# A fused sketch-attention and MoE kernel: two loads issued later, a transpose moved, GpSimd products gated behind VectorE, and a new placement of the attention steps between the MoE waves

## The chip, the cores and the metric

The kernel runs on one core of one Trainium2 chip. The metric is device time in microseconds for one launch; lower is better. The engines of the core work side by side, each through its own instruction queue in program order: TensorE (PE in the profile, its weight loads as PEld), VectorE (DVE), ScalarE (ACT), GpSimd (POOL) and SyncE (SP), which here issues nearly all DMA transfers.

## The reference

Two stages, and the second one takes the output of the first.

```python
def phi(x):                       # r = 8 sketches, their outer product: 64 features
    a = np.einsum('rd,bhsd->bhsr', S1, x)
    b = np.einsum('rd,bhsd->bhsr', S2, x)
    return np.einsum('bhsi,bhsj->bhsij', a, b).reshape(*x.shape[:-1], r * r)

q_p, k_p = phi(q), phi(k)         # q, k, v: (4 batches, 4 heads, 1088 rows, 32)
kv = np.einsum('bhsf,bhsd->bhfd', k_p, v)
z = np.sum(k_p, axis=2)
num = np.einsum('bhsf,bhfd->bhsd', q_p, kv)
den = np.einsum('bhsf,bhf->bhs', q_p, z)[..., None] + 1e-06
attn = num / den

x = attn.transpose(0, 2, 1, 3).reshape(4352, 128)
h = x @ w_in                      # w_in: (128, 2048)
g = h * (1.0 / (1.0 + np.exp(-beta * h)))
out = g @ w_out                   # w_out: (2048, 128)
```

All inputs and the output are float32.

## The kernel before

**Attention, one batch at a time.** The 1088 rows of a head are cut into 34 blocks of 32 rows, called u. `k_turn` and `q_turn` (L313, L319) transpose the loaded k and q on VectorE in 32 by 32 blocks; `k_project` and `q_project` (L338) apply both sketches on TensorE into two PSUM banks of the tag "att", and two VectorE transposes (L349) bring the result back as `ab`. `k_product` (L365) forms the outer products of k, one part on VectorE and one on GpSimd; `v_copy` (L326) puts v into the layout that `kv` (L384, TensorE) needs. `kv_spread` (L394, L398), `weights` (L408, L416) and `kv_repeat` (L426 on TensorE, L434 on ScalarE) turn kv and z into operands. `den_rows` (L440) and `den_product` (L454 to L459) with `den_invert` and `weigh` (L470, L471, L486) give q's factors divided by the denominator, `an`. Then for each of three chunks of the batch `q_multiply` (L504, a product) and `q_back` (L512, a transpose) make the features of q, and `num` (L524) multiplies them with kv on TensorE. `evacuate` (L585) writes the result to `x_all` in fp16.

The first chunk of batch 0 goes another way, so that its x is there early: its numerator is made without the division (`num_first`, copied to `ns` at L548), the reciprocals are spread by a selector matrix on TensorE (`quotient`, L556), and a VectorE product (L565) joins both into `x_all`. In this chunk `q_multiply(0)` and `q_back(0)` do not need the denominator.

**MoE in waves.** The 136 blocks of all batches are cut into ten chunks of 12, 11, 11, then six of 16, and 6 blocks. beta is folded into the weights: `winp` is w_in times beta (GpSimd, L276), `woutp` is w_out over beta (GpSimd L291, ScalarE L285). A chunk of the first nine has eight waves. A wave is two first matmuls (L635) into a pair of PSUM banks ("wave", two such pairs), one ScalarE activation (L642) to `gT`, and, two waves later, two second matmuls (L611) into the accumulator bank. A chunk ends with a VectorE transpose (L616) and its stores (L622).

**Order.** It is written out by hand; no scheduler moves anything. Up to the first wave the order is the source order (L643 to L720). From then on a table `plan` has one dictionary for each batch: the number behind a step is its due time in waves. After wave n (waves counted from 1) every step whose due time is below n is issued, in order of due time. Every engine gets its instructions in that order, so a step that is issued early stands in front of later work in its queue, and a wait in it holds up all that is behind. Slots that are not in the table are not run.

**Loads.** A `load_…` first puts a small memset on the destination (`hold`, L120), which ties the load to that point of VectorE's queue, and then issues the transfer on SP's queue. SP takes its transfers in order, so one that waits for its memset holds back the ones behind it.

**Gates.** `in_turn(one, other)` writes the same small tile `gate` on two engines, one after the other (L126, L127); the second engine goes on only when the first one has got there.

**Fillers.** `warm(n)` issues n matmuls on a tile of zeros (L221) whose result is not used; they stand in TensorE's queue in program order. `kv`, `k_project`, `q_project`, `kv_repeat`, `den_rows` and `num_part` all take banks of the two "att" ones, so each has to wait until the reader of the bank's last tile is done.

Of the kernel before, what the change touches and what calls it, by code (L numbers as in the profile page):

```python
# [18 lines left out]
def kernel(  # L19
# [19 lines left out]
    nc = tc.nc  # L39
# [10 lines left out]
    C = 9  # L50
# [58 lines left out]
    UH = U // 2 + 1  # L109
# [9 lines left out]
    def hold(eng, t):  # L119
        eng.memset(t[:, 0:1], 0.0)  # L120
# [4 lines left out]
    def in_turn(one, other):  # L125
        one.memset(gate, 0.0)  # L126
        other.memset(gate, 0.0)  # L127

    def load_w_in():
        nc.sync.dma_start(out=w_in_sb, in_=moe_w_in)  # L130
        nc.sync.dma_start(out=betat, in_=moe_beta.rearrange("(p j) -> p j", j=NJ))
# [5 lines left out]
    def load_k(b, eng, u0=0, u1=U):  # L137
        hold(eng, k_in[b][:, u0 * D : u1 * D])
        nc.sync.dma_start(out=k_in[b][:, u0 * D : u1 * D], in_=k_rows[b][:, u0 * D : u1 * D])

    def load_q(b, eng):
        hold(eng, q_in[b])
        nc.sync.dma_start(out=q_in[b], in_=q_rows[b])

    def load_v_late(b, eng):
        hold(eng, v_in[b].rearrange("p h c d -> p (h c d)"))
        load_v(b)
# [71 lines left out]
    def warm(n):  # L219
        for _ in range(n):  # L220
            nc.tensor.matmul(  # L221
                out=idle_out[:, 0:NI], lhsT=idle[:, 0:P], rhs=idle[:, 0:NI], start=True, stop=True
            )
# [50 lines left out]
    def scale_w_in(j0, j1):  # L274
        for j in range(j0, j1, 2):
            nc.gpsimd.tensor_tensor(  # L276
                out=winp[:, j : j + 2, :],
                in0=apx(w_in_sb, j, [[1, 2], [NJ, P]]),
                in1=apx(beta_bc, j * P, [[P, 2], [1, P]]),
                op=ALU.mult,  # L280
            )

    def scale_w_out_act(j0, j1):
        for j in range(j0, j1):
            nc.scalar.activation(  # L285
                out=woutp[:, j, :], in_=w_out_sb[:, j, :], func=ACTF.Copy, scale=rbetat[:, j : j + 1]
            )
# [364 lines left out]
    at = [Attention(b) for b in range(B)]  # L652
    a0 = at[0]
# [7 lines left out]
    sketch_rows()  # L661
    warm(2)
    a0.k_project((0, 1))
    load_k(1, nc.vector, 0, UH)
    load_w_in()
    a0.k_turn((1,))
    a0.k_project((2, 3))
    warm(10)
# [3 lines left out]
    for i in range(2):  # L672
# [2 lines left out]
    sketch_columns()  # L675
    warm(3)
    a0.k_product(nc.vector, 0, 4)
    in_turn(nc.vector, nc.gpsimd)
    a0.q_turn()
    a0.k_product(nc.gpsimd, 7, C)  # L680
# [8 lines left out]
    a0.q_multiply(0)  # L689
    load_w_out(nc.vector)  # L690
    in_turn(nc.vector, nc.gpsimd)
    a0.q_back(0)
    scale_w_in(0, 10)
    warm(2)
    load_k(1, nc.vector, UH, U)
# [3 lines left out]
    a0.kv_repeat((0,))  # L699
    a0.den_rows(0, 1)  # L700
    a0.kv_repeat((1,))
    at[1].k_turn((0,))
    a0.den_product(0, 1)
    a0.den_invert(0, 1, rz[:, :, 0:H])
    a0.spread_rden()
    nc.vector.reciprocal(out=rbetat, in_=betat)
    a0.num_first()
    warm(3)
    a0.quotient()
    load_v_late(1, nc.vector)  # L710
    a0.den_rows(1, NCH, idle_out[:, NI:512])
# [10 lines left out]

    slots = []
    plan = [
        {"wo3": 1, "wo5": 2.3, "wo7": 6.1, "mul1": 0.4, "back1": 1.8, "mul2": 0.45, "back2": 1.85, "num": 5.65, "ev": 5.7},
        {"turn_k": 3.5, "proj_k": 6.4, "vcopy": 5.1, "kp_pool": 9.1, "turn_q": 3.8, "kp": 6.65, "proj_q": 7.2, "kv0": 9.15, "kv1": 9.2, "spread": 9.25, "weights": 9.3, "repeat": 18.4, "den": 9.35, "inv": 9.4, "mul0": 12.65, "back0": 15.3, "mul1": 15.3, "back1": 15.65, "mul2": 15.75, "back2": 18.1, "num": 22.5, "ev": 22.55},
        {"load_k": 0, "load_q": 3.65, "load_v": 14, "turn_k": 7.8, "turn_q": 11.95, "vcopy": 20.3, "proj_k": 19.15, "kp_pool": 23.35, "kp": 20, "proj_q": 23.3, "kv0": 24.6, "kv1": 24.65, "spread": 25.3, "weights": 26.95, "repeat": 35.4, "den": 27, "inv": 27.45, "mul0": 28.1, "back0": 32.05, "mul1": 31.55, "back1": 33.2, "mul2": 33.1, "back2": 36.15, "num": 38.65, "ev": 38.7},
        {"load_k": 16.4, "load_q": 8.7, "load_v": 29.6, "turn_k": 23.4, "turn_q": 24.45, "vcopy": 36.6, "proj_k": 37.55, "kp_pool": 40.5, "kp": 38.2, "proj_q": 39, "kv0": 41.85, "kv1": 41.9, "spread": 43.35, "weights": 43.4, "repeat": 49.1, "den": 44.05, "inv": 45.1, "mul0": 48.25, "back0": 49.2, "mul1": 48.3, "back1": 50.75, "mul2": 50.65, "back2": 54.3, "num": 54.65, "ev": 54.85},
    ]
    for b, steps in enumerate(plan):  # L730
        a = at[b]
        ch0 = 1 if b == 0 else 0
        do = {
            "load_k": lambda b=b: load_k(b, nc.vector),
            "load_q": lambda b=b: load_q(b, nc.vector),
            "load_v": lambda b=b: load_v_late(b, nc.vector),
            "turn_k": lambda a=a, b=b: a.k_turn((1,) if b == 1 else (0, 1)),
            "turn_q": a.q_turn,
            "vcopy": lambda a=a: a.v_copy(nc.gpsimd.tensor_copy),
            "proj_k": a.k_project,  # L740
            "proj_q": a.q_project,
            "kp_pool": lambda a=a: a.k_product(nc.gpsimd, 6, C),
            "kp": lambda a=a: a.k_product(nc.vector, 0, 6),
            "kv0": lambda a=a: a.kv((0,)),
            "kv1": lambda a=a: a.kv((1,)),
            "spread": a.kv_spread,
            "weights": a.weights,
            "repeat": a.kv_repeat,
            "den": lambda a=a: (a.den_rows(0, NCH), a.den_product(0, NCH)),
            "inv": a.weigh,  # L750
            "num": lambda a=a, ch0=ch0: a.num_part(ch0, NCH),
            "ev": lambda a=a, b=b: a.evacuate("VVAA" if b else "AVAA"),
        }
        for ch in range(NCH):
            do[f"mul{ch}"] = lambda a=a, ch=ch, e=nc.gpsimd if b == 1 and ch == 1 else None: a.q_multiply(ch, e)
            do[f"back{ch}"] = lambda a=a, ch=ch: a.q_back(ch)
        for i in range(NJ // 2):
            do[f"wo{i}"] = lambda i=i: scale_w_out_act(2 * i, 2 * i + 2)
        slots += [(w, b, do[step]) for step, w in steps.items()]
# [39 lines left out]
```

## Time and profile before

| | |
|---|---|
| median of 3 runs | 111.91 us (111.76 to 112.13) |
| the profiled execution's own time | 113.0 us |
| its span, first to last instruction | 111.3 us |
| mean granted TensorE clock | 0.978 |
| PE busy | 101.0 us (91%) |
| ACT busy | 76.4 us (69%) |
| DVE busy | 69.3 us (62%) |
| POOL busy | 27.8 us (25%) |
| first wave starts | 19.02 us |
| last ScalarE activation starts | 106.30 us |

The page gives busy times and a picture of the span in 40 slices of 2.78 us; a digit is the busy share of a slice in tenths. Matmuls overlap in the records, so a full PE row says that TensorE was never without work, and not that the work could not be denser. The chain of waits goes back from the last instruction to what released it. In a row of the timeline the first number is the start in us, the second the busy time of the group; a bracket gives the idle time of the engine in front of it and what ended it. Releasers are inferred from semaphores.

By the waits of TensorE from 46 us on, it stands still once, for 0.2 us. Its waits from 19 to 46 us sum to 4.6 us: 1.7 for VectorE's transposes in front of kv, 1.5 for ScalarE in three places, 0.7 for zi, 0.4 for the transposed q products, 0.3 for wc.

### The profile page before, as it was taken

The numbers are of one execution on the slowest core, as the hardware profiler recorded it, in microseconds if no ns is written. First come the engines' busy times: TensorE is split into PE (matmuls) and PEld (weight loads), VectorE is DVE, ScalarE is ACT, GpSimd is POOL, SyncE is SP. The second block draws the span as 40 slices with busy tenths as digits, with TensorE's granted clock in tenths as the row PEclk, the third lists the DMA queues.
The fourth block names the chain that finished last, engine by engine and source line by source line (L and its number), as shares of the span: only waits on it lengthen the run. The fifth ranks groups of instructions, "written<-read, shape, count | busy, mean of one in ns | idle before, by whom it ended". The sixth has DMA issues, their size and how long they took to land.

```text
span 111.3 us, 3316 instructions
## 1 busy us (share of the span) xinstructions
PE 101.0 (91%) x1401; PEld 50.1 (45%) x1401; DVE 69.3 (62%) x136; ACT 76.4 (69%) x110; POOL 27.8 (25%) x55
## 2 busy tenths in 40 slices
PE   5998999669936999999999999999999999999960
PEld 3443865324433555446344434463443444444640
DVE  5569984996895799969589949434998220020120
ACT  0704512995620499753979986757999799999940
POOL 6505299934500050590000038200000000000000
PEclk9999999999997699999999999999999999999997
DMA  3999498575004506740221720022004105004143
GB/s 85 300 236 342 138 333 337 162 222 194 34 0 142 135 0 185 203 87 9 38 32 54 193 47 6 0 51 49 0 4 69 28 0 95 2 9 72 19 71 59
DMA packets 22407, 11.25 MB, mean 101 GB/s; under 512 B 18804, under 2 KB 20852, under 8 KB 22136
## 3 DMA queue, kind: packets, MB, share of 16 engines
q1 hardware_dynamic: 21936, 10.97, 37.3%
q8 instruction: 11, 0.18, 0.7%
q10 hardware_dynamic: 456, 0.06, 0.3%
q14 instruction: 4, 0.03, 0.1%
HBM read 8.80 MB, written 2.23 MB: 99 GB/s over the span
## 4 chain that ended last, share of the span: by engine, by line
PE 58%; ACT 18%; DVE 12%; DMA 6%; issue 2%; SPq 1%; DVEq 0%
PE wave L635 19%; PE acc L611 17%; ACT gT L642 16%; DMA q_in<-in_q_dram 6%; PE wave L524 5%; PE att L338 4%; DVE kp L365 2%; PE att L384 2%; PE att L440 2%; PE wave L384 2%; PE att L426 2%; PE acc L221 2%; DVE qp L504 2%; DVE qpt L512 2%; PE att L524 1%
## 5 line engine op out<-in xcount | busy, mean ns | idle before, releaser
L642 ACT ACTIVATE gT<-wave 128x1024 f16<-128x1024 f32 (+2 forms) x76 | 65.6, 954 | 15.3 <-PE wave L635 15.2
L635 PE MATMUL wave<-x_all,winp 128*128 128x512 f16 (+3 forms) x160 | 42.3, 351 | 1.5 <-ACT gT L642 1.5
L611 PE MATMUL acc<-gT,woutp 128*128 128x512 f16 (+3 forms) x160 | 42.0, 349 | 0.2 <-ACT gT L642 0.2
L635 PEld LDWEIGHTS <-winp 128*128 128x128 f16 x160 | 14.0, 99 | 22.0 <-issue 12.6
L611 PEld LDWEIGHTS <-woutp 128*128 128x128 f16 x160 | 15.5, 98 | 14.6 <-issue 0.4
L616 DVE STREAM_TRANSPOSE osb<-acc 128x512 f32<-128x512 f32 (+3 forms) x10 | 6.3, 630 | 18.2 <-PE acc L611 18.2
L326 POOL COPY vc<-v_in 96x256 f32<-96x256 f32 (+2 forms) x8 | 6.2, 810 | 21.5 <-DMA v_in<-in_v_dram 21.5
L512 DVE STREAM_TRANSPOSE qpt<-qp 128x768 f32<-128x768 f32 x12 | 11.1, 953 | 0.0
L349 DVE STREAM_TRANSPOSE ab<-att 128x288 f32<-128x288 f32 x16 | 6.7, 458 | 4.7 <-PE att L338 4.6
L221 PE MATMUL acc<-idle 128*128 128x320 f16 x39 | 8.0, 346 | 1.3 <-DVE idle L156 1.3
L365 DVE TENSOR_TENSOR kp<-ab 128x1536 f32<-128x1536 f32 (+2 forms) x5 | 8.6, 1727 | 0.7 <-DVE ab L349 0.5
L365 POOL TENSOR_TENSOR kp<-ab 128x768 f32<-128x768 f32 (+1 forms) x4 | 7.2, 1791 | 4.6 <-DVE ab L349 4.6
L504 DVE TENSOR_TENSOR qp<-an,ab 128x768 f32<-128x768 f32 x8 | 7.7, 984 | 0.1
L524 PE MATMUL wave<-qpt,kvw 32*32 32x288 f32 (+2 forms) x192 | 7.3, 344 | 0.5 <-DVE qpt L512 0.4
L276 POOL TENSOR_TENSOR winp<-w_in_sb,beta_bc 128x256 f16<-128x256 f32 x8 | 6.6, 846 | 0.7 <-DMA w_in_sb<-in_moe_w_in_dram 0.7
L313 DVE STREAM_TRANSPOSE kT<-k_in 128x576 f32<-128x576 f32 (+1 forms) x8 | 5.6, 715 | 1.0 <-DMA k_in<-in_k_dram 1.0
L524 PE MATMUL att<-qpt,kvw 32*32 32x288 f32 (+1 forms) x128 | 6.1, 392 | 0.0
L384 PE MATMUL att<-vc,kp 128*32 128x33 f32 x432 | 4.3, 198 | 1.7 <-DVE ab L349 1.7
L221 PEld LDWEIGHTS <-idle 128*128 128x128 f16 x39 | 3.8, 111 | 4.4 <-DVE idle L156 1.3
L524 PEld LDWEIGHTS wave<-qpt,kvw 32*32 32x32 f32 x192 | 4.0, 103 | 3.2 <-ACT gT L642 1.5
L319 DVE STREAM_TRANSPOSE qT<-q_in 128x1088 f32<-128x1088 f32 x4 | 5.2, 1296 | 0.1
L384 PEld LDWEIGHTS att<-vc,kp 128*32 128x32 f32 x432 | 4.0, 108 | 2.8 <-issue 2.8
(97 smaller groups left out, 77.2 us busy)
## 6 DMA issues: line engine op xcount, KB each, us to landing
q_in<-in_q_dram SPq DMA_DIRECT2D x4, 544.0 KB, 4.7
v_in<-in_v_dram SPq DMA_DIRECT2D x12, 144.0 KB, 2.8
k_in<-in_k_dram SPq DMA_DIRECT2D x2, 544.0 KB, 4.0
w_in_sb<-in_moe_w_in_dram SPq DMA_DIRECT2D x1, 1024.0 KB, 8.1
w_out_sb<-in_moe_w_out_dram SPq DMA_DIRECT2D x1, 1024.0 KB, 4.8
out_dram<-osb SPq DMA_DIRECT2D x16, 64.0 KB, 2.0
k_in<-in_k_dram SPq DMA_DIRECT2D x2, 288.0 KB, 2.9
k_in<-in_k_dram SPq DMA_DIRECT2D x2, 256.0 KB, 3.8
```

Of the source, the lines that this page charges most:

```text
L221: nc.tensor.matmul(out=idle_out[:, 0:NI], lhsT=idle[:, 0:P], rhs=idle[:, 0:NI], start=True, stop=True)
L276: nc.gpsimd.tensor_tensor(out=winp[:, j : j + 2, :], in0=apx(w_in_sb, j, [[1, 2], [NJ, P]]), in1=apx(beta_bc, j * P, [[P, 2], [1, P]]), op ...
L349: nc.vector.transpose(out=apx(ab, T * p, [[2 * T, C], [1, T]]), in_=banks[p][:, 0 : C * T])
L365: eng.tensor_tensor(out=apx(self.kp, c0 * H * F, [[F, n], [R, R], [1, R]]), in0=apx(t, c0 * H * 2 * R, [[2 * R, n], [1, R], [0, R]]), in1= ...
L384: nc.tensor.matmul(out=self.kvp[m * g : m * g + m, r * self.kvs : r * self.kvs + D + 1], lhsT=self.kp[:, c * H + h, f0 : f0 + m], rhs=self ...
L504: (eng or nc.vector).tensor_tensor(out=apx(qp, 0, [[F, n], [R, R], [1, R]]), in0=a, in1=apx(self.ab, c0 * H * 2 * R + R, [[2 * R, n], [0, ...
L512: nc.vector.transpose(out=apx(self.qpt, ch * CW * T, [[T, CW], [C * T, 2 * H], [1, T]]), in_=self.qp[ch].rearrange("p n f -> p (n f)"),)
L524: nc.tensor.matmul(out=banks[s][T * h : T * h + T, 0:n], lhsT=self.kvw[T * s : T * s + T, h % 2, fb, h // 2, :], rhs=self.qpt[T * s : T * ...
L611: nc.tensor.matmul(out=acc[:, :n], lhsT=woutp[:, j, :], rhs=gT[:, j, :n], start=(j == 0), stop=(j == NJ - 1))
L616: nc.vector.transpose(out=osb[:, :un, :].rearrange("p u m -> p (u m)"), in_=acc[:, :n])
L635: nc.tensor.matmul(out=wave[:, jj // (nj // 2), jj % (nj // 2) * n : (jj % (nj // 2) + 1) * n], lhsT=winp[:, j0 + jj, :], rhs=x, start=Tru ...
L642: nc.scalar.activation(out=gT[:, j0 : j0 + nj, :n].rearrange("p (i k) n -> p i k n", i=2), in_=wave[:, :, : nj // 2 * n].rearrange("p i (k ...
```

## The change

Six things, all in the order in which work is issued; no computation is added or left out.

1. In the head, the load of the first half of batch 1's k and the loads of w_in and betat are issued behind VectorE's first k product, and no longer between the two halves of batch 0's k projection.
2. `q_back(0)` of batch 0 goes from in front of `kv_spread` to behind wc (the end of `weights`), where batch 1's first `k_turn` was; that goes behind rbetat.
3. The three fillers between `num_first` and `quotient` are taken out.
4. GpSimd's part of the k product of each later batch (`kp_pool`) gets a gate in front: it starts only when VectorE has got to the same place in its queue.
5. Chunk 1 of batch 1's q product, which GpSimd makes in both kernels, has a step of its own (`pool1`) with such a gate.
6. All due times of the table are new. The steps of batch 1 between kv and inv, which were due at 9.15 to 9.4, are due at 9.45 to 11.9; `proj_k` of batch 1 comes ahead of batch 0's `num`, and `proj_q` of batch 2 ahead of batch 1's `num`.

```diff
@@ -661,8 +661,6 @@
     sketch_rows()
     warm(2)
     a0.k_project((0, 1))
-    load_k(1, nc.vector, 0, UH)
-    load_w_in()
     a0.k_turn((1,))
     a0.k_project((2, 3))
     warm(10)
@@ -675,6 +673,8 @@
     sketch_columns()
     warm(3)
     a0.k_product(nc.vector, 0, 4)
+    load_k(1, nc.vector, 0, UH)
+    load_w_in()
     in_turn(nc.vector, nc.gpsimd)
     a0.q_turn()
     a0.k_product(nc.gpsimd, 7, C)
@@ -689,7 +689,6 @@
     a0.q_multiply(0)
     load_w_out(nc.vector)
     in_turn(nc.vector, nc.gpsimd)
-    a0.q_back(0)
     scale_w_in(0, 10)
     warm(2)
     load_k(1, nc.vector, UH, U)
@@ -699,13 +698,13 @@
     a0.kv_repeat((0,))
     a0.den_rows(0, 1)
     a0.kv_repeat((1,))
-    at[1].k_turn((0,))
+    a0.q_back(0)
     a0.den_product(0, 1)
     a0.den_invert(0, 1, rz[:, :, 0:H])
     a0.spread_rden()
     nc.vector.reciprocal(out=rbetat, in_=betat)
+    at[1].k_turn((0,))
     a0.num_first()
-    warm(3)
     a0.quotient()
     load_v_late(1, nc.vector)
     a0.den_rows(1, NCH, idle_out[:, NI:512])
@@ -722,10 +721,10 @@
 
     slots = []
     plan = [
-        {"wo3": 1, "wo5": 2.3, "wo7": 6.1, "mul1": 0.4, "back1": 1.8, "mul2": 0.45, "back2": 1.85, "num": 5.65, "ev": 5.7},
-        {"turn_k": 3.5, "proj_k": 6.4, "vcopy": 5.1, "kp_pool": 9.1, "turn_q": 3.8, "kp": 6.65, "proj_q": 7.2, "kv0": 9.15, "kv1": 9.2, "spread": 9.25, "weights": 9.3, "repeat": 18.4, "den": 9.35, "inv": 9.4, "mul0": 12.65, "back0": 15.3, "mul1": 15.3, "back1": 15.65, "mul2": 15.75, "back2": 18.1, "num": 22.5, "ev": 22.55},
-        {"load_k": 0, "load_q": 3.65, "load_v": 14, "turn_k": 7.8, "turn_q": 11.95, "vcopy": 20.3, "proj_k": 19.15, "kp_pool": 23.35, "kp": 20, "proj_q": 23.3, "kv0": 24.6, "kv1": 24.65, "spread": 25.3, "weights": 26.95, "repeat": 35.4, "den": 27, "inv": 27.45, "mul0": 28.1, "back0": 32.05, "mul1": 31.55, "back1": 33.2, "mul2": 33.1, "back2": 36.15, "num": 38.65, "ev": 38.7},
-        {"load_k": 16.4, "load_q": 8.7, "load_v": 29.6, "turn_k": 23.4, "turn_q": 24.45, "vcopy": 36.6, "proj_k": 37.55, "kp_pool": 40.5, "kp": 38.2, "proj_q": 39, "kv0": 41.85, "kv1": 41.9, "spread": 43.35, "weights": 43.4, "repeat": 49.1, "den": 44.05, "inv": 45.1, "mul0": 48.25, "back0": 49.2, "mul1": 48.3, "back1": 50.75, "mul2": 50.65, "back2": 54.3, "num": 54.65, "ev": 54.85},
+        {"wo3": 2.7, "wo5": 0.8, "wo7": 2.2, "mul1": 1.4, "back1": 1.95, "mul2": 1.75, "back2": 2.5, "num": 6.25, "ev": 6.3},
+        {"turn_k": 1.1, "proj_k": 4.1, "vcopy": 8.8, "kp_pool": 4.85, "turn_q": 5.1, "kp": 7.05, "proj_q": 7.5, "kv0": 9.45, "kv1": 9.5, "spread": 10.25, "weights": 10.9, "repeat": 15.6, "den": 11.45, "inv": 11.9, "mul0": 12.25, "back0": 14, "back1": 19.6, "mul2": 17.8, "back2": 20.35, "num": 22.4, "ev": 22.95, "pool1": 12.9},
+        {"load_k": 3, "load_q": 6.25, "load_v": 10.8, "turn_k": 8.6, "turn_q": 11.25, "vcopy": 18.2, "proj_k": 16.75, "kp_pool": 19.2, "kp": 21.1, "proj_q": 20.9, "kv0": 23.1, "kv1": 23.15, "spread": 24.2, "weights": 24.95, "repeat": 36, "den": 26.8, "inv": 27.85, "mul0": 29.3, "back0": 31.65, "mul1": 33.95, "back1": 35.8, "mul2": 35.1, "back2": 36.15, "num": 38.05, "ev": 38.1},
+        {"load_k": 16.2, "load_q": 11.7, "load_v": 29, "turn_k": 30, "turn_q": 25.05, "vcopy": 37.6, "proj_k": 37.15, "kp_pool": 38.2, "kp": 37.3, "proj_q": 39.3, "kv0": 40.15, "kv1": 40.2, "spread": 41.35, "weights": 43.4, "repeat": 53.5, "den": 44.05, "inv": 44.5, "mul0": 46.85, "back0": 46.9, "mul1": 48.6, "back1": 48.65, "mul2": 51.65, "back2": 54.3, "num": 54.35, "ev": 54.7},
     ]
     for b, steps in enumerate(plan):
         a = at[b]
@@ -739,7 +738,7 @@
             "vcopy": lambda a=a: a.v_copy(nc.gpsimd.tensor_copy),
             "proj_k": a.k_project,
             "proj_q": a.q_project,
-            "kp_pool": lambda a=a: a.k_product(nc.gpsimd, 6, C),
+            "kp_pool": lambda a=a: (in_turn(nc.vector, nc.gpsimd), a.k_product(nc.gpsimd, 6, C)),
             "kp": lambda a=a: a.k_product(nc.vector, 0, 6),
             "kv0": lambda a=a: a.kv((0,)),
             "kv1": lambda a=a: a.kv((1,)),
@@ -752,7 +751,8 @@
             "ev": lambda a=a, b=b: a.evacuate("VVAA" if b else "AVAA"),
         }
         for ch in range(NCH):
-            do[f"mul{ch}"] = lambda a=a, ch=ch, e=nc.gpsimd if b == 1 and ch == 1 else None: a.q_multiply(ch, e)
+            do[f"mul{ch}"] = lambda a=a, ch=ch: a.q_multiply(ch)
+            do[f"pool{ch}"] = lambda a=a, ch=ch: (in_turn(nc.vector, nc.gpsimd), a.q_multiply(ch, nc.gpsimd))
             do[f"back{ch}"] = lambda a=a, ch=ch: a.q_back(ch)
         for i in range(NJ // 2):
             do[f"wo{i}"] = lambda i=i: scale_w_out_act(2 * i, 2 * i + 2)
```

## The prediction

> **What bounds the kernel now.** I read the page's slices first (40 slices of 2.78 us):
>
> ```profile
> PE   5998999669936999999999999999999999999960
> ACT  0704512995620499753979986757999799999940
> PEclk9999999999997699999999999999999999999997
> ```
>
> From slice 16 on TensorE (PE) is full; from 88 us ScalarE (ACT) is full as well. Nothing the change does there can shorten it unless the work itself shrinks, and it does not. Before that there are holes: slices 7, 8 and 11, and a lower clock in slices 12 and 13. So the change is worth what it takes out of the first 52 us. The timeline of TensorE alone shows the hole of slice 11 (start, duration, instruction, in brackets the idle time before it and what ended it):
>
> ```profile
> 30.27 0.49 PE L611 MATMUL acc<-gT,woutp 128*128 128x384 f16 x2
> 32.45 1.42 PE L384 MATMUL att<-vc,kp 128*32 128x33 f32 x144 [1.69 <-DVE ab L349]
> 34.56 0.55 PE L408 MATMUL att<-zi,s2rep 128*128 128x32 f32 x2 [0.69 <-DVE zi L394]
> 35.39 1.19 PE L440 MATMUL att<-qT,wc 128*32 128x288 f32 x8 [0.28 <-DVE wc L416]
> 36.51 0.77 PE L635 MATMUL wave<-x_all,winp 128*128 128x352 f16 x2
> ...
> 38.47 0.46 PE L635 MATMUL wave<-x_all,winp 128*128 128x352 f16 x2
> ```
>
> Between 30.76 and 36.51 no MoE wave runs: batch 1's kv, weights and den are all due between waves 10 and 11 (9.15 to 9.35), so TensorE sits through every VectorE (DVE) step between them. Waves are counted from 1 here, batches from 0. The windows of one us show what follows (busy us per engine, clock, DMA share, GB/s):
>
> ```profile
> 31.00:32.00 1.00, 0.00 (x0) 0.00 (x0) 1.00 (x2) 0.25 (x1) 0.00 (x0) 1.00 0.00 0
> 35.00:36.00 1.00, 0.72 (x9) 0.20 (x8) 0.19 (x1) 0.00 (x0) 0.00 (x0) 0.50 0.87 292
> 37.00:38.00 1.00, 1.00 (x5) 0.50 (x4) 0.93 (x3) 0.69 (x1) 0.00 (x0) 0.50 0.76 123
> ```
>
> The granted clock is 0.50 there, and the two waves at 36.51 and 37.66 take 1.96 us together, against about 0.65 each from 38.47 on. The 1.69 us has its own cause, in the timelines of VectorE and GpSimd (POOL):
>
> ```profile
> 28.79 1.51 POOL L365 TENSOR_TENSOR kp<-ab 128x768 f32<-128x768 f32 x1 [2.50 <-DVE ab L349]
> 29.16 2.74 DVE L365 TENSOR_TENSOR kp<-ab 128x1536 f32<-128x1536 f32 x1 [0.53 <-DVE ab L349]
> 31.83 0.83 DVE L349 STREAM_TRANSPOSE ab<-att 128x288 f32<-128x288 f32 x2
> ```
> ```profile
> 67.10 1.76 DVE L365 TENSOR_TENSOR kp<-ab 128x1536 f32<-128x1536 f32 x1
> 67.14 3.08 POOL L365 TENSOR_TENSOR kp<-ab 128x768 f32<-128x768 f32 x1 [2.09 <-DVE ab L349]
> ```
>
> Whichever product starts first runs at its own length (1.51, 1.76) and the other one waits it out: 28.79 + 1.51 = 30.30, and 30.30 to 31.90 is about one clean VectorE product. The batch 1 product loses 0.98 us to this. Lastly the head, from the chain:
>
> ```profile
> 1.72 7.01 DMA q_in<-in_q_dram
> ...
> 17.07 0.51 PE acc L221 x3
> 17.59 0.62 PE att L556 x8
> ```
>
> **The change part by part.** Profiled run: 113.0 us, of which 111.3 are span and 1.7 lie around it; the plain runs' median, 111.91, is 1.1 below it. I work out the saving in span and take it off the median.
>
> *Loads later.* q lands at 8.73, but VectorE is only free at 8.67 (product at 7.44, then the gate's memset), so q earlier is worth at most 0.06, and the hold's memset (0.06) now stands right there: 0. v lands earlier (ScalarE's copy at 10.71 had waited 0.92), but kv at 11.51 stands behind four fillers that end at about 11.58: 0. On SP's queue k (288 KB) and w_in go out at about 8.8 and 9.2 instead of 5.15 and 5.54; betat behind them; w_out waits for its own hold at 12.92 as before. w_in took 8.1 us to land among q and v, w_out, the same size, 4.8. I take 4.8, nearest since q and v are then down, plus 0.7 for k ahead of it (288 KB at the 403 GB/s of 10 to 11 us): 14.7 against 13.64. GpSimd's first five winp products take 4.07, the first woutp 0.61: ready at 19.5. Wave 3's turn needs that at about 20.3 (20.73 less the 0.4 below), so 0.8 us covers it. With 8.1 it lands at 17.3, and woutp is 1.8 late: upper bound +1.8, lower 0.
>
> *q transpose behind W, fillers.* VectorE's q_back (0.98) takes the place of the k turn (0.77) behind wc: the denominator's chain ends 0.2 later, at 17.03, just under the end of num_first on TensorE (17.07). The three fillers (0.51) go, so the selector starts at 17.08 and ends at 17.70. The k turn (0.77) now stands between rbetat (16.95 to 17.16) and the quotient, to 17.9: x_all starts then and not at 18.30. First wave 0.4 earlier (bounds 0 and 0.5).
>
> *Chunk 0.* VectorE does the second k turn (0.67) ahead of the two q products, and batch 1's two transposes (0.85) ahead of batch 0's num, which wants the att banks they free. Batch 0's num: 24.91 − 0.4 + 0.67 + 0.7 (the 0.85 less the slack the old start had) = 25.9. In return batch 1's projection is done. GpSimd's product runs 25.9 to 27.4 under VectorE's q turn, a transpose (at 38.97 one of 1.30 ran its length beside a GpSimd product). Then GpSimd's v copy (0.9 for its first piece, of 1.29) holds VectorE's product to 28.3, which then takes 1.76: 30.05. Bounds: 0 if VectorE gets in first, 1.29 if both pieces go ahead. kv needs one att bank, free after the first q transpose (0.43): 30.5, against 32.45: **−1.95**.
>
> *Batch 1's steps, spread out.* Between the end of kv (33.87) and the wave after den (36.51) lie 2.64 us without a wave. Now kv ends at 31.9; wave 11 (0.65) fits under VectorE's k turn (1.32) and output transpose (0.57), which stand ahead of zi, weights starts at 33.0, wave 12 follows, den (0.65 at full clock) ends at 34.7. By then waves 11 and 12 are done, so the next, wave 13, starts at 34.7 instead of 38.47: **−3.8** in all, of which 0.65 is the clock that no longer drops. The repeat moves from wave 19 to 16: same work (0.42), hidden by nothing, no difference.
>
> *Given back.* Batch 2's q projection is now ahead of batch 1's num, so num waits for VectorE's two transposes. VectorE's queue has no slack from 20.7 to 45.6: q turn to 34.9, cc to an 2.3, three products and three transposes 0.95 each, projections' transposes 0.85 twice, an output 0.55: 44.15. TensorE is there at 43.65: **+0.5**. Bounds: 0, and 1.4 if GpSimd's v copy of batch 2 takes its 0.9 from VectorE's second product. The four new gates are memsets of 0.06 on VectorE that start while the neighbour ends (one at 25.31 inside the transpose at 25.29): 0, at most 0.2.
>
> *From wave 26 (52.20) on* the same work follows as before: num, repeat and kv of batch 3 lie within a wave or four of where they were, GpSimd's last product waits for VectorE (behind the x copies, 69.6 on the old clock, done 71.2, and kv needs its part only at about 72). 0; the cover is a full TensorE; without it up to 1.5.
>
> Sum: −3.8 + 0.5 = −3.3; batch 2's weights (0.1 to 0.4) are already done by then where they were not before: **−3.4**, span 107.9, time 111.91 − 3.4 = 108.5. With the bounds of the parts: +0.5 +1.8 at the bad end (−1.1), −4.2 at the good one.
>
> A rule to weigh: by the one-us windows (0.84 in 34 to 35, 0.50 in the next three, 0.95 in 38 to 39) the clock was halved from 34.7 to 38.1, though the longest empty stretch before is 1.69 us. The Trainium skill (TensorE: Matmul & The Clock Gate, Part 1) says that it takes a whole idle window of some 3.4 us, and as long a busy one to come back. The return agrees (3.4 us at half); the fall does not quite, unless the narrow kv counts as idle. By the page nothing in the new order could drop the clock; by the row a hole of under 2 us might.
>
> **Rivals.**
> 1. *The clock falls elsewhere.* ScalarE's four woutp scalings after wave 3 leave TensorE waiting some 0.75 us at 23.6, weights 0.45, num 0.5. For: 22 to 24 us are already only 0.53 to 0.61 busy, now with k projections nearer. Against: those did not drop it. A drop of 3.4 us at 0.50 costs up to 1.7: 110.2. With the w_in bound instead: 108.5 + 1.8 = 110.3.
> 2. *Slower: VectorE becomes the bound.* GpSimd's five pieces of batches 1 and 2 (1.51 + 1.29 + 1.51 + 1.29 + 1.51 = 7.1 us) now lie under a VectorE queue without slack. If they hold up transposes too, and not products alone, each us comes out at num of batch 1; I counted 0.9. It decides from 4.3 us of the 7.1 on; all of it gives 108.5 + 6.2 = 114.7, half of the rest 111.6. For: v copy and product at 45.71 and 46.27 stretched each other (2.81, 2.00). Against: the transpose at 38.97.
> 3. *It does not do what it says:* GpSimd still meets VectorE and the hole at kv just moves behind the att banks, +1.95 and the clock's 0.65 with weights' wait: 108.5 + 3.3 = 111.8, no change.
>
> **How the numbers follow.** Forecast 0.63 (its own range 107.7 to 109.5), rival 1 0.18, rival 2 0.14, rival 3 0.05. About 0.3% is what a measurement of this kernel can tell from no change. Rival 2 has little that is not slower; I leave 0.13 slower, 0.05 same, 0.82 faster. The range takes in the good end (−4.2 gives 107.7, less 0.3 for what weights and fillers may add) and rival 1 up to 110.8; outside are most of rivals 2 and 3.
>
> **What would show it.** Right: no wait of 1.69 before kv of batch 1, kv near 30.5; GpSimd's product 1.51 and VectorE's 1.76 side by side with transposes; clock 1.00 from 33 to 39; first wave near 18.6; wave 26 near 49; a wait of about 0.5 at batch 1's num. Wrong: winp or woutp waiting for w_in beyond 15.7, a clock of 0.50 anywhere, num of batch 1 later than 46, or holes after 50 us, where I put nothing.

## The result, and the profile after

| | before | after |
|---|---|---|
| median | 111.84 us (111.75 to 112.13, 4 runs) | 108.60 us (108.38 to 109.48, 4 runs) |
| ratio after / before | | 0.9721 (95% interval 0.9665 to 0.9778) |
| the profiled execution's own time | 113.0 us | 108.38 us |
| its span | 111.3 us | 106.7 us |
| mean granted TensorE clock | 0.978 | 1.0 |
| first wave starts | 19.02 us | 18.61 us |
| wave 26 starts | 52.20 us | 47.61 us |

The kernel became faster by 3.2 us; 108.5 was predicted. A few executions of several kernels below came out 1 to 4% above the others of the same kernel; the ratios leave them out.

The slices of the after kernel, 2.67 us each, with the same rows as before:

```profile
PE   5999999689979999999999999999999999999950
ACT  0705412897736977558999947597998799999940
PEclk9999999999999999999999999999999999999999
```

Slice 11 (counted from 0), a 3 before, is now a 7, and the clock row has no dip. The timeline of TensorE in the after kernel, from the end of chunk 0's waves on:

```profile
29.27 0.49 PE L611 MATMUL acc<-gT,woutp 128*128 128x384 f16 x2
30.31 1.53 PE L384 MATMUL att<-vc,kp 128*32 128x33 f32 x144 [0.55 <-DVE ab L349]
31.77 0.47 PE L635 MATMUL wave<-x_all,winp 128*128 128x352 f16 x2
...
32.38 0.40 PE L408 MATMUL att<-zi,s2rep 128*128 128x32 f32 x2
32.62 0.46 PE L635 MATMUL wave<-x_all,winp 128*128 128x352 f16 x2
...
33.31 0.69 PE L440 MATMUL att<-qT,wc 128*32 128x288 f32 x8
33.93 0.47 PE L635 MATMUL wave<-x_all,winp 128*128 128x352 f16 x2
...
47.61 0.60 PE L635 MATMUL wave<-x_all,winp 128*128 128x512 f16 x2
```

kv of batch 1 starts at 30.31 and not at 32.45, its wait is 0.55 us and not 1.69, and a wave stands between each two of the narrow steps (kv, spread, den). Wave 13 is at 33.93 where it was at 38.47, and wave 26, the last row, at 47.61 where it was at 52.20. The one-us windows of the after kernel at the places of the dip (busy us per engine, clock, DMA share, GB/s):

```profile
35.00:36.00 1.00, 1.00 (x8) 0.57 (x6) 0.94 (x4) 1.00 (x3) 0.00 (x0) 1.00 0.50 80
37.00:38.00 1.00, 1.00 (x18) 0.49 (x20) 0.97 (x3) 0.96 (x4) 0.41 (x2) 1.00 1.16 269
```

TensorE is busy all the time, at a clock of 1.00. Batch 1's k product, in the timelines of VectorE and GpSimd of the after kernel:

```profile
25.52 1.30 DVE L319 STREAM_TRANSPOSE qT<-q_in 128x1088 f32<-128x1088 f32 x1
...
27.50 2.27 DVE L365 TENSOR_TENSOR kp<-ab 128x1536 f32<-128x1536 f32 x1
```
```profile
25.76 1.51 POOL L365 TENSOR_TENSOR kp<-ab 128x768 f32<-128x768 f32 x1
27.21 2.82 POOL L326 COPY vc<-v_in 128x896 f32<-128x896 f32 x2
```

GpSimd's product now runs beside a VectorE transpose, and both keep their length (1.30 and 1.51). What is left of the meeting is GpSimd's v copy (2.82 for two pieces) against VectorE's product (2.27, where 1.76 is its own length).

From wave 26 to the end both profiled executions take the same: 111.3 − 52.20 = 59.1 and 106.7 − 47.61 = 59.1 us. All the gain lies ahead of that point. But 4.6 us are gained there between the two profiles and only 3.2 between the medians; a second profile of the kernel before (the last experiment) explains the difference.

### The profile page after: what moved, and what is told of

It is laid out like the page before. It is cut to its first block, busy times and chain, and to the rows that moved or that the text cites. A ratio compares the mean times of both kernels' runs of the same rounds, so it can differ in the third digit from the quotient of the medians.

```text
span 106.7 us, 3318 instructions
## 1 busy us (share of the span) xinstructions
PE 99.2 (93%) x1398; PEld 49.6 (46%) x1398; DVE 68.6 (64%) x140; ACT 76.2 (71%) x110; POOL 28.1 (26%) x59
## 4 chain that ended last, share of the span: by engine, by line
PE 66%; ACT 22%; DVE 6%; issue 2%
PE wave L635 20%; ACT gT L642 19%; PE acc L611 17%; PE acc L221 5%; PE wave L524 5%; PE att L338 4%; PE att L384 4%; DVE kp L365 3%; PE att L524 2%; PE wave L384 2%; PE att L426 2%; PE att L440 2%; ACT woutp L285 2%; DVE qT L319 1%; DVE ab L349 1%
## 5 line engine op out<-in xcount | busy, mean ns | idle before, releaser
L635 PE MATMUL wave<-x_all,winp 128*128 128x512 f16 (+3 forms) x160 | 41.7, 347 | 1.4 <-ACT gT L642 1.4
L326 POOL COPY vc<-v_in 96x256 f32<-96x256 f32 (+2 forms) x8 | 7.9, 1014 | 14.9 <-DMA v_in<-in_v_dram 14.9
L365 DVE TENSOR_TENSOR kp<-ab 128x1536 f32<-128x1536 f32 (+2 forms) x5 | 8.0, 1605 | 0.1
L524 PE MATMUL wave<-qpt,kvw 32*32 32x288 f32 (+2 forms) x192 | 7.8, 344 | 0.1
L524 PE MATMUL att<-qpt,kvw 32*32 32x288 f32 (+1 forms) x128 | 6.6, 392 | 0.0
L127 POOL MEMSET gate<- 128x1 f32 x6 | 0.6, 99 | 20.6 <-DVE gate L126 19.2
L365 POOL TENSOR_TENSOR kp<-ab 128x768 f32<-128x768 f32 (+1 forms) x4 | 5.6, 1400 | 0.0
L585 ACT CAST x_all<-att 128x288 f16<-128x288 f32 (+1 forms) x8 | 2.6, 384 | 3.2 <-PE att L524 3.2
```

The lines of the kernel that those rows point to most:

```text
L326: f(out=self.vc[0:p1, c0:c1, :, 0:D].rearrange("p c h d -> p h c d"), in_=v_in[self.b][0:p1, :, c0:c1, :],)
L365: eng.tensor_tensor(out=apx(self.kp, c0 * H * F, [[F, n], [R, R], [1, R]]), in0=apx(t, c0 * H * 2 * R, [[2 * R, n], [1, R], [0, R]]), in1= ...
L524: nc.tensor.matmul(out=banks[s][T * h : T * h + T, 0:n], lhsT=self.kvw[T * s : T * s + T, h % 2, fb, h // 2, :], rhs=self.qpt[T * s : T * ...
L635: nc.tensor.matmul(out=wave[:, jj // (nj // 2), jj % (nj // 2) * n : (jj % (nj // 2) + 1) * n], lhsT=winp[:, j0 + jj, :], rhs=x, start=Tru ...
```

## The experiments

Each ratio is against the kernel before on the same chip (medians there 111.91, 111.78 and 112.11). The after kernel was measured a second time in the last group: 108.66 us (108.31 to 109.41, 6 runs), ratio 0.9702 (0.9662 to 0.9742).

**The head alone** (e1_head): the kernel before, with points 1 to 3 of the change and the old table.

```diff
     a0.k_project((0, 1))
-    load_k(1, nc.vector, 0, UH)
-    load_w_in()
...
     a0.k_product(nc.vector, 0, 4)
+    load_k(1, nc.vector, 0, UH)
+    load_w_in()
...
-    a0.q_back(0)
...
-    at[1].k_turn((0,))
+    a0.q_back(0)
...
+    at[1].k_turn((0,))
     a0.num_first()
-    warm(3)
```

> The head of the new kernel (loads later, q transpose behind W, no fillers ahead of the selector) with the old table and no new gates. My theory: the head is worth 0.4 us, all of it from the fillers, and it passes through to the end: 111.5 us, first wave at 18.6 and not 19.0. Rival: the head is the larger part of the 3.2 us (q and v earlier): 109.5 or less. Second rival: the later waits swallow it: 111.9.

Four executions: 111.02, 114.22, 114.59 and 114.59 us, so no ratio: inconclusive. The first lies 0.5 below the expected 111.5, which is nearer than either rival. In the profiled one (114.59) w_out landed 7.4 us after its issue, TensorE waited 1.2 us for woutp, and the clock was 0.50 between 35 and 41 us. Both come back below.

**Table and gates alone** (e2_plan): the old head with points 4 to 6.

```diff
-        {"wo3": 1, "wo5": 2.3, "wo7": 6.1, "mul1": 0.4, ...
+        {"wo3": 2.7, "wo5": 0.8, "wo7": 2.2, "mul1": 1.4, ...
...
-            "kp_pool": lambda a=a: a.k_product(nc.gpsimd, 6, C),
+            "kp_pool": lambda a=a: (in_turn(nc.vector, nc.gpsimd), a.k_product(nc.gpsimd, 6, C)),
```

> The old head with the new table and the new gates. My theory: all but 0.4 us of the gain is here: 109.0 us, kv of batch 1 near 30.7, no half clock. Rival (head is the larger part): 111.0 or more.

108.88 us (108.74 to 109.32), ratio 0.9709 (0.9652 to 0.9765). By the ratios the whole gain is here (0.9721 and 0.9702 for the after kernel). The medians (108.60 and 108.66 against 108.88) and the two spans (106.7 against 107.0) leave some 0.3 us for the head, which the intervals, about 0.6 us to each side, do not tell from nothing.

**The spread alone** (e3_spread): the kernel before with four due times of batch 1 as in the after kernel.

```diff
-        ... "spread": 9.25, "weights": 9.3, "repeat": 18.4, "den": 9.35, "inv": 9.4, ...
+        ... "spread": 10.25, "weights": 10.9, "repeat": 18.4, "den": 11.45, "inv": 11.9, ...
```

> The kernel before with only batch 1's steps behind kv spread out (spread 10.25, weights 10.9, den 11.45, inv 11.9). Theory: the 2.64 us without a wave behind kv fill up, wave 13 starts up to 2.2 us earlier than 38.47, but VectorE's queue is as long as before, and num of batch 1 needs the att banks that its transposes free at about 46.2, so most comes back as a wait in front of num: 0.7 to 1.0 us faster, 111.0 us. Rival: the holes behind kv were the loss itself, and the gain passes through: 109.7 us. On the clock: the 1.69 us hole in front of kv is still there; if it alone halves the clock, 0.50 is seen again near 35 to 38 us; by the page's rule of a whole idle window it is not.

112.25 us (111.88 to 112.39, 10 runs), ratio 1.0008 (0.9981 to 1.0036): nothing. TensorE's waits for zi and wc (0.7 and 0.3) are gone from its profile, yet the end does not move. VectorE shows why; first the kernel before (its second profile, e13_before), then e3_spread:

```profile
36.08 0.48 DVE L457 STREAM_TRANSPOSE cc<-att 128x288 f32<-128x288 f32 x1 [0.81 <-PE att L440]
...
44.00 0.93 DVE L512 STREAM_TRANSPOSE qpt<-qp 128x768 f32<-128x768 f32 x1
44.86 0.80 DVE L349 STREAM_TRANSPOSE ab<-att 128x288 f32<-128x288 f32 x2
...
47.59 0.81 DVE L585 CAST x_all<-wave 128x288 f16<-128x288 f32 x2
```
```profile
36.53 0.48 DVE L457 STREAM_TRANSPOSE cc<-att 128x288 f32<-128x288 f32 x1 [1.06 <-PE att L440]
...
44.45 0.93 DVE L512 STREAM_TRANSPOSE qpt<-qp 128x768 f32<-128x768 f32 x1
45.31 0.80 DVE L349 STREAM_TRANSPOSE ab<-att 128x288 f32<-128x288 f32 x2
...
47.83 0.81 DVE L585 CAST x_all<-wave 128x288 f16<-128x288 f32 x2
```

VectorE's cc starts 0.45 later: 0.2 of that stands already at kv (32.73 against 32.52), and 0.25 comes from the waves in front of `den_rows`, for which cc now waits 1.06 and not 0.81. From there on VectorE has no gap, and qpt and ab are 0.45 late as well. The MoE waves had moved ahead by some 0.9 us (wave 14 at 37.00, which was at 37.91), but then TensorE stands in front of num of batch 1:

```profile
45.53 0.67 PE L524 MATMUL wave<-qpt,kvw 32*32 32x288 f32 x4 [0.62 <-ACT gT L642]
```

Num reads qpt, which VectorE has ready at 44.45 + 0.93 = 45.38. The releaser that is put down, a ScalarE activation, ends at 45.41, but it is not what num needs: in e13_before num starts at 45.70, and the same activation ends only at 46.27. Num also needs the two att banks, which VectorE's ab transposes free 0.45 late, so the wave behind num starts at 47.66 and not at 47.24. So one hole of TensorE was filled and another opened behind it, where VectorE's queue is late.

**The collision alone** (e4_gate): the kernel before, with batch 1's GpSimd product behind VectorE's.

```diff
-        {"turn_k": 3.5, ... "kp_pool": 9.1, ...
+        {"turn_k": 3.5, ... "kp_pool": 6.7, ...
...
-            "kp_pool": lambda a=a: a.k_product(nc.gpsimd, 6, C),
+            "kp_pool": lambda a=a, b=b: (b == 1 and in_turn(nc.vector, nc.gpsimd), a.k_product(nc.gpsimd, 6, C)),
```

> The kernel before with one thing: GpSimd's product of batch 1 gated behind VectorE's (due 6.7 and a gate). Theory (two products exclude each other, VectorE's queue is what sets num of batch 1): VectorE's product 1.76 and not 2.74, GpSimd's 1.51 behind it, kv near 31.0 and not 32.45, and about 1.2 us faster: 110.7 us. Rival: GpSimd's product is then late for kv's last third, or the hole moves behind kv: 111.8 us.

111.48 us (110.93 to 111.76, 10 runs), ratio 0.9937 (0.9909 to 0.9965): 0.7 us, and 1.2 was expected. TensorE, VectorE and GpSimd in its profile:

```profile
32.13 0.62 PE L384 MATMUL att<-vc,kp 128*32 128x33 f32 x48 [0.69 <-DVE ab L349]
33.32 1.03 PE L384 MATMUL att<-vc,kp 128*32 128x33 f32 x96 [0.57 <-POOL kp L365]
```
```profile
29.83 1.76 DVE L365 TENSOR_TENSOR kp<-ab 128x1536 f32<-128x1536 f32 x1 [0.51 <-DVE ab L349]
```
```profile
31.76 1.51 POOL L365 TENSOR_TENSOR kp<-ab 128x768 f32<-128x768 f32 x1
```

VectorE's product is back at 1.76, but kv starts only 0.4 earlier (32.13, where 31.0 was expected), and GpSimd's product is now behind VectorE's, so TensorE waits a second time (0.57), for the last part of kv. VectorE's wait of 0.51 in front of its product is still there, so it is not GpSimd's product that causes it. In the after kernel GpSimd goes first, under a transpose; no run here takes that order alone.

**The spread taken out of the new order** (e9_unspread): the after kernel with those four steps close together again.

```diff
-        ... "spread": 10.25, "weights": 10.9, "repeat": 15.6, "den": 11.45, "inv": 11.9, ...
+        ... "spread": 9.55, "weights": 9.6, "repeat": 15.6, "den": 9.65, "inv": 9.7, ...
```

> The new kernel with batch 1's spread, weights, den and inv put back directly behind kv (9.55 to 9.7), the rest new. Theory (VectorE's queue and TensorE bind together from 19 to 46 us): TensorE loses the two waves that fit between (0.9) and VectorE waits for den without the q turn to fill it (0.7), and both pass through: 109.4 us. Rival (the spreading is worth nothing, as alone in the kernel before): 108.6 us.

Ratio 0.9834 (0.9787 to 0.9882) against 0.9702 to 0.9721 for the after kernel, so the spread is worth 1.2 to 1.5 us in the new order. Its six executions took 109.50, 109.62, 110.15, 110.94, 111.14 and 112.36 us; the fastest is 1.2 above the after kernel's 108.31. The profile is that of 111.14, and part of what it lost is not the spread's: kv of batch 1 starts 1.35 later there than in the after kernel (31.66), behind a wait of TensorE of 1.1 for woutp and one of VectorE of 1.2 for batch 1's k. Num of batch 1 starts 2.41 later (45.39 against 42.98), so 1.06 arises between the two. The waits for zi (0.6) and wc (0.3) are back on TensorE, and VectorE again waits 0.82 for cc. The same four numbers that did nothing in the old order are worth over 1 us here.

**Without the gates** (e5_nogate): the after kernel without `in_turn` in `kp_pool` and `pool1`.

```diff
-            "kp_pool": lambda a=a: (in_turn(nc.vector, nc.gpsimd), a.k_product(nc.gpsimd, 6, C)),
+            "kp_pool": lambda a=a: a.k_product(nc.gpsimd, 6, C),
...
-            do[f"pool{ch}"] = lambda a=a, ch=ch: (in_turn(nc.vector, nc.gpsimd), a.q_multiply(ch, nc.gpsimd))
+            do[f"pool{ch}"] = lambda a=a, ch=ch: a.q_multiply(ch, nc.gpsimd)
```

> The new kernel without its four new gates; all due times stay. Theory: where the steps stand does the work, not the gates: GpSimd's products of batches 1 and 2 are issued in front of VectorE's and start with the transposes anyhow, and only batch 3's meets VectorE's product again (3.08 and 1.76 as before), under a full TensorE: 108.6 us, no change. Rival: the gates are what removes the collisions: 109.5 or more.

Six executions: 108.11, 109.06, 109.24, 110.32, 110.63 and 112.60 us. The ratio of the first three, 0.9723 (0.9675 to 0.9770), shows no loss, and 108.11 is the fastest execution of all. But the other three lie above all ten of the after kernel, so that the gates are worth nothing is not shown. The profile is that of 112.60: w_out landed 8.4 us after its issue, TensorE waited 1.7 us for woutp and then ran at half clock from 24 to 27 us, VectorE waited 1.3 us for batch 1's k, and TensorE stood for 1.71 us in the middle of kv for a reason that the profile does not show. GpSimd's k product of batch 1 takes 1.51 without its gate too, and batch 3's meets VectorE's again (3.08, against 1.51 with the gate), both as expected. Its q product of batch 1 takes 2.28 beside one of VectorE's, against 1.51. So the gates do prevent two meetings, but ones that only GpSimd paid for: VectorE's products, which went first, took their own 1.76 and 0.96.

**w_in later still** (e6_late): the load of w_in and betat behind VectorE's second k product, 1.7 us further on (issued at 11.03 and not at 9.33).

```diff
     load_k(1, nc.vector, 0, UH)
-    load_w_in()
     in_turn(nc.vector, nc.gpsimd)
...
     a0.k_product(nc.vector, 4, 7)
+    hold(nc.vector, w_in_sb)
+    load_w_in()
```

> The new kernel with w_in and betat issued another 2.1 us later, behind VectorE's second k product. Theory: the first woutp pair was ready at 19.53 and wanted at 20.32, so 0.8 us are covered; 2.1 later TensorE waits 1.3 us or more for GpSimd in front of its first second matmul, more if w_out is then held up behind w_in: 110.0 us (109.6 to 110.8). Rival: the loads have much more cover than that, since later waits swallow it: 108.6 us.

108.78 us (108.39 to 109.96), ratio 0.9754 (0.9705 to 0.9803). The expected 110.0 was wrong: against the after kernel that is 0.1 to 0.2 us by the medians and 0.4 to 0.6 by the ratios, with intervals that overlap. In the profile of 108.39 winp starts at 16.19 and not 14.73, and TensorE does wait for woutp, 0.8 us in two pieces; but its wait for ScalarE's gT falls from 1.4 to 0.6 us. In that execution the wait only changed its name.

**No fillers** (e8_nofill): the after kernel without the nine fillers that are left in the first stage behind batch 0's q projection.

```diff
     a0.q_project()
-    warm(4)
...
     scale_w_in(0, 10)
-    warm(2)
...
-    warm(3)
     a0.den_product(1, NCH)
```

> The new kernel without the nine fillers that are left between the q projection and the first wave (four before kv of batch 0, two behind it, three before the first wave). Theory: they stand in the way like the three that were taken out; kv starts 0.6 earlier, the first wave 0.8, and w_in just keeps up: 107.8 us. Rival: they hold the clock up, and a half clock of 3.4 us costs up to 1.7: 108.6 to 109.5 us. Second rival: winp and woutp bind at once: 108.4 us.

109.96 us (109.27 to 112.11), ratio 0.9805 (0.9770 to 0.9841): slower than the after kernel, not faster. The first wave does come earlier (17.71). TensorE and a two-us window of its profile:

```profile
21.28 0.74 PE L611 MATMUL acc<-gT,woutp 128*128 128x384 f16 x2 [1.70 <-POOL woutp L291]
```
```profile
22.00:24.00 2.00, 2.00 (x8) 0.97 (x7) 2.00 (x4) 2.00 (x6) 2.00 (x4) 0.50 0.11 33
```

w_out is late (landed 7.7 us after its issue), TensorE waits 1.70 us for woutp, and then runs at half clock (0.50 for all of 22 to 24 us, and 0.85 and 0.80 in the windows on either side). VectorE waits as well, 1.8 us for the second half of batch 1's k. The earlier first wave only makes the wait for woutp longer.

**The after kernel again** (e10_after), beside two variants with a later load of batch 1's q.

> The new kernel once more, beside the next two on one chip. Theory: w_out's landing decides what an execution takes: 4.8 to 5.8 us after its issue the time is 108.4 to 108.8, from some 6.5 on TensorE waits for woutp and it is 109.5 or more, as in the profiles of the last four runs (6.3 to 8.4). Rival: the spread of times has nothing to do with it.

The times are above. Its profiled execution was 109.41, a us over the first one. GpSimd in it, beside the same instruction in the first profile of the after kernel:

```profile
20.60 1.18 POOL L291 TENSOR_TENSOR woutp<-w_out_sb,rbetat 128x256 f16<-128x256 f32 x2 [1.98 <-DMA w_out_sb<-in_moe_w_out_dram]
```
```profile
18.92 1.19 POOL L291 TENSOR_TENSOR woutp<-w_out_sb,rbetat 128x256 f16<-128x256 f32 x2
```

w_out landed 7.5 us after its issue here and 5.8 there. TensorE waits 0.8 us for woutp here and not at all there. VectorE waits 0.8 us here too, and not there, for the second half of batch 1's k, which is issued right behind w_out and landed 8.1 us after its issue (6.0 in the first profile); kv of batch 1 starts at 31.17 and not at 30.31. The ten runs of this kernel lie in two groups, 108.31 to 108.73 (seven) and 109.31 to 109.48 (three); that the landing of w_out and k parts them rests on one profile of each. The profiles of e2_plan, e6_late and e11_q_late fit it: w_out landed after 4.9, 6.3 and 5.4 us, VectorE did not wait for k, and they took 108.74, 108.39 and 108.60.

**q later** (e11_q_late): the load of batch 1's q behind rbetat, so that it does not share the queue with w_out.

```diff
     a0.kv_spread()
-    load_q(1, nc.vector)
     a0.weights()
...
     nc.vector.reciprocal(out=rbetat, in_=betat)
+    load_q(1, nc.vector)
```

> The new kernel with batch 1's q load moved from behind kv_spread to behind rbetat (some 2.8 us later), so that it does not share the wires with w_out. Theory: w_out lands 4.8 to 5.8 us after its issue each time, TensorE does not wait for woutp, 108.4 us with less spread; q lands near 23 and is wanted at 25.5. Rival: k's second half alone delays w_out as much, or q comes late: 109 us or more.

108.64 us (108.40 to 110.06), ratio 0.9700 (0.9658 to 0.9742): the median of the after kernel, and no smaller spread. w_out landed after 5.4 us and nothing waited for it, in this one profile.

**q later and no fillers** (e12_q_late_nofill): both edits together.

> The same without the nine fillers. Theory: the fillers were not holding up the clock; it fell because TensorE waited 1.7 us for woutp. With w_out in time the first wave starts near 17.7, nothing waits, and the 0.8 comes through: 107.8 us. Rival: without fillers the clock falls anyhow: 109.3 us or more.

109.28 us (108.37 to 109.69), ratio 0.9734 (0.9687 to 0.9780). Again no gain over the after kernel, and w_out again landed late (7.9 us after its issue; TensorE waited 1.7 us), though q's load was out of its way; VectorE waited 2.2 us for k. So w_out lands late without q as well.

**The kernel before again** (e13_before): a second profile of it.

> The kernel before once more, for a profile at full clock. Theory: the half clock in the profile of before is no part of its usual time (one run of 19 showed it): span near 110.2, no 0.50 near 36 us, and TensorE, which then has waves 11 and 12 done 0.6 to 1.1 earlier, waits for num of batch 1, whose start stays within 0.7 us of 46.96. Rival: the half clock is there each time: span 111.3.

111.78 us, span 110.0, clock 1.00. TensorE, and the window of the dip:

```profile
32.52 1.42 PE L384 MATMUL att<-vc,kp 128*32 128x33 f32 x144 [1.69 <-DVE ab L349]
34.63 0.41 PE L408 MATMUL att<-zi,s2rep 128*128 128x32 f32 x2 [0.69 <-DVE zi L394]
35.32 0.69 PE L440 MATMUL att<-qT,wc 128*32 128x288 f32 x8 [0.28 <-DVE wc L416]
...
37.27 0.46 PE L635 MATMUL wave<-x_all,winp 128*128 128x352 f16 x2
...
50.95 0.60 PE L635 MATMUL wave<-x_all,winp 128*128 128x512 f16 x2
```
```profile
37.00:38.00 1.00, 1.00 (x8) 0.57 (x6) 0.93 (x3) 1.00 (x3) 0.00 (x0) 1.00 1.12 180
```

The hole before kv and the two behind it are the same as in the profile shown first, but the clock does not fall. Wave 13 starts at 37.27 and wave 26 at 50.95, both 1.2 us earlier than in that profile. The dip was 1.2 us of one execution. Against this cleaner profile the after kernel gains 50.95 − 47.61 = 3.3 us up to wave 26, which is what the medians show. Num starts at 45.70, with no wait: the expectation, which had TensorE wait and num stay within 0.7 us of 46.96, was wrong in that.

By median or ratio no variant was faster than the after kernel beyond the intervals.

## Why the prediction was right

The time was right to 0.1 us, and most steps came where the prediction put them; that it was so close is partly luck, as three errors nearly cancel. Point by point:

**Loads later, 0: right, with a cover that was misread.** winp starts at 14.73 and the first woutp at 18.92, done by 19.5, as predicted. The cover may be larger than the 0.8 us that I gave it: with w_in 1.7 us later still nothing was lost that the intervals show, and in that profile ScalarE's waits take up what woutp is late. What the prediction did not see are the transfers behind. w_out is still issued at 13.0, when the DMA engines are now full: they moved 426 GB/s from 12 to 13 us in the after profile, 94 in the one before. w_out landed 4.8, 4.8, 4.9, 5.7 and 6.6 us after its issue in the five profiles with the old place of the loads, and 5.8, 7.4, 7.5, 7.7, 7.8 and 8.4 in the six with the new one; with w_in later still it was 6.3, and with q out of the way 5.4 and 7.9. In the six where it took 7.4 us or more, TensorE waited 0.8 to 1.7 us for woutp. In the five of these with the new table VectorE also waited 0.8 to 2.2 us for the second half of batch 1's k, which the new table wants earlier (its turn is due at 1.1 and not at 3.5). The medians hide this. That the full DMA engines are what delays w_out is argued and not shown: in e11_q_late they moved 410 GB/s in the same us, and w_out landed after 5.4.

**First wave 0.4 earlier: right, and of little worth.** 18.61 against 19.02. What the head as a whole brings, some 0.3 us, can't be told from nothing.

**kv of batch 1 at 30.5: right.** 30.31, with VectorE's product of 27.50 to 29.77 held by GpSimd's v copy. I expected the product to start at 28.3 and take 1.76; it started ahead of the copy's end and took 2.27, to nearly the same effect.

**The steps spread out, −3.8: mis-sized on both sides.** The prediction counted from wave 13 at 38.47, in the profile with the dip, and put 0.65 of the 3.8 down to the clock. The dip is not in the usual execution, so it can't be saved there, and its whole size is 1.2 us (38.47 against 37.27) and not 0.65. On the other side wave 13 came at 33.93, 0.8 earlier than the 34.7 that was forecast. Against the clean profile wave 13 starts 3.3 us earlier (37.27 − 33.93), against the shown one 4.5. The prediction had noticed that the profiled execution was 1.1 us above the median, and did not ask where in the trace that 1.1 us was.

**Given back, +0.5 at num of batch 1: it did not happen.** The prediction's terms for VectorE's queue up to there add up to 45.15 as they are written, and not to 44.15; they count three products of batch 1, of which GpSimd makes one, and with two they give about 44.2. In the after profile the q turn ends at 34.23 and not at 34.9, the transposes in front of num start at 42.32 and end at 43.13, and num starts at 42.98 with no wait.

So three errors nearly cancel. Without the dip, with the earlier wave 13 and without the 0.5, the prediction's terms give −3.8 + 1.2 − 0.8 = −3.4, or −3.5 with the 0.1 that it counts for batch 2's weights; it had −3.4, and the clean profile shows −3.3 at wave 26. What kept the dip out of the time was that the saving was taken off the median: the forecast of the span, 107.9, was 1.2 too long (106.7), and wave 26, forecast near 49, came at 47.61.

**From wave 26 on, 0: right.** 59.1 us in each shown profile, 59.05 in the clean one (110.0 − 50.95).

The mechanism was right in its place and too simple. I followed TensorE's holes, but between 36 and 47 us VectorE is as full as TensorE: in the clean profile before, 3.98 of 4 us from 39 to 43 and 3.97 from 43 to 47. So a hole that is filled on TensorE pays only if VectorE's chain from den to num also comes earlier. e3_spread shows that directly: 1.0 us of TensorE's waits taken out, nothing gained. What VectorE itself waits for, from 20 to 47 us in the kernel before (e13_before), and then from 20 to 46 in the after kernel (us in total, times, longest):

```profile
DVE ab L349 <- PE att L338: 0.9, 1, 0.9
DVE cc L457 <- PE att L440: 0.8, 1, 0.8
DVE kp L365 <- DVE ab L349: 0.5, 1, 0.5
DVE wc L416 <- PE att L408: 0.3, 1, 0.3
```
```profile
DVE x_all L585 <- ACT x_all L585: 0.4, 1, 0.4
DVE wc L416 <- PE att L408: 0.3, 1, 0.3
```

2.5 us became 0.7. Num, up to which this counts, starts at 45.70 and 42.98; in the after kernel VectorE waits again behind it, 1.19 us up to 46.83 for batch 2's kv, while TensorE is full. The projection of batch 1's k is done early, so its transposes find their input there (0.9). VectorE's product no longer comes directly behind the transposes that it reads, since batch 1's q turn stands between them (0.5). GpSimd's product no longer stands in its way, so that it takes 2.27 and not 2.75. And the q turn of batch 2 (1.30) now stands where VectorE waited for the denominators (0.8), which is why the spread costs VectorE nothing in the new order: e9_unspread loses 1.2 us and gets the wait for cc back. That these gains need each other is shown for the spread (0 alone, over 1 in company); the early projection was not tried alone. Num starts 2.7 us earlier in the after kernel, and batch 2's q projection (0.7), which used to come behind it, is then already done: these make up the 3.3 us at wave 26.

**The rivals.** The first, a clock that falls elsewhere, is not in the after kernel's profile, but it exists: in e8_nofill, e12_q_late_nofill and e5_nogate it falls to 0.50 within 1.3 us after the 1.7 us wait for woutp. The second, that GpSimd holds up VectorE's transposes too, is refuted by the transpose of 1.30 beside GpSimd's product of 1.51. The third, that nothing moves, fell with the result.

On the clock: the same three holes (1.69, 0.69 and 0.28 us) stand in both profiles of the kernel before and in e1_head. The clock fell behind them in the first (0.50 from 34.7 to 38.1) and in e1_head (0.50 from 35 to 41), and not in the second. It fell after a single wait of 1.7 us in e8_nofill, e12_q_late_nofill and e5_nogate, and not after one of 1.1 (e9_unspread) or 0.8 (e10_after). The Trainium skill's rule (TensorE: Matmul & The Clock Gate, Part 1), which the prediction weighed, is a whole idle window of about 3.4 us, whose phase is not tied to the kernel's start. A window with a phase of its own would explain that the same holes lower the clock in one execution and not in another. But the longest empty stretch of TensorE was 1.7 us in all of these, and the fall came all the same. What counts as idle stays open.

Open too is why w_out lands anywhere between 4.8 and 8.4 us after its issue. Without the nine fillers the clock does fall nearly every time: eleven of the twelve executions of e8_nofill and e12_q_late_nofill have a mean clock of 0.984 or less, all ten of the after kernel one of 0.992 or more. Whether the fillers keep it up by being work, or by holding the first wave back so that the wait for woutp is shorter, stays open; e5_nogate, which has all its fillers, shows the same fall after the same wait. And the lower clock does not always cost time: e12_q_late_nofill's fastest execution, 108.37 us, has a mean clock of 0.968.

## What to carry to other kernels

When two engines are both full over a stretch, filling one engine's holes can merely open another hole behind the other engine's queue, as in e3_spread; look for what the second one waits for, and put work of its own there. Before counting what a profile shows as a saving, compare the profiled execution with the median: if it is slower, find the place in the trace that makes it so, and leave that out of the sum. A load that is issued later is not finished with when its own data are in time: it may still fill the DMA engines when the next loads are issued, and those can then come late.

## What the runs showed of the hardware

Of a GpSimd product and a VectorE product of two SBUF tiles that meet, the second waits out the first, to some 0.2 us: 1.51 and 2.74 where GpSimd went first, 1.76 and 3.08 where VectorE did. GpSimd's v copy, with one input, takes part as well: its two pieces took 2.82 beside a product and 1.28 without one (e5_nogate). VectorE's transposes (1.30 beside a GpSimd product) and its products with one input in PSUM do not take part: batch 0's two from 21.29 took 1.78, no more than the 0.92 to 0.96 each of later ones, beside two of GpSimd's scalings at their usual length (1.66, that is 0.83 each). The Trainium skill (SBUF — State Buffer, Who interferes with whom) says the same: an exclusive lock on a shared port, which a VectorE instruction with two SBUF inputs needs against a GpSimd instruction that reads SBUF, and one with at most one SBUF input does not, outside VectorE's two-port modes. The rows named here agree.

The half clock comes and goes between executions of one kernel: of 41 plain runs of the kernel before in three groups, two had a mean clock of 0.978 or less (113.13 and 115.14 us), and the other 39 of 0.991 or more. With the new head and the old table (e1_head) three of four had 0.97 (114.22 to 114.59 us), and one 1.00 (111.02).
